# Gate and up of a gated feed-forward block from seven block products per pair of token tiles, with combined weights prepared during attention

## The chip, the cores and the metric

The kernel runs on one core of a Trainium2 chip. The metric is the device time of one launch in microseconds (us); the table below has three runs of it. PE is TensorE, DVE VectorE, ACT ScalarE, POOL GpSimd, SP the engine that issues the DMAs.

## The reference

A transformer layer in float32 on 2048 tokens of width 512: attention with 32 heads of 16 in a sliding window of 256, then a feed-forward part of width 1376 whose gate is a sigmoid.

```
h  = x + attention(layernorm(x), wqkv, wo)
n  = layernorm(h)
h2 = h + (sigmoid(n @ w_gate) * (n @ w_up)) @ w_down
```

## The kernel before

**Tiling.** There are 16 token tiles of 128 (`NT`) and 4 k-tiles of 128 (`KT`). The feed-forward width is cut into columns of 512, 512 and 352 (`CUTS`, L49), called cut 0, 1 and 2 here. To keep float32 accuracy, each operand of the large products is scaled and split into two float16 numbers, hi and lo, and `mm3` (L290 to L293) adds three matmuls for each k-tile: hi·hi, hi·lo and lo·hi. A weight piece is split by `do_split` (L789): ACT writes hi (L796), DVE writes lo (L799).

**Stages.** At first the attention weights are loaded and split (`prep`), x goes into `X`, which stays in SBUF as the residual, and layernorm and the projections of the first tokens run. Attention then goes over 8 blocks of 256 tokens: scores for the row maximum (`do_s`, L593, and the maximum on DVE, L578), scores with keys on partitions (`do_st`, L647 to L658), exponentials on ACT (L623), masks on POOL (L631, L636), the product with the values (`do_pv`, L684), and the output projection, which adds to `X` (`do_wo`, L752). Keys reach their copies through a DRAM buffer (`SK<-mem`). During attention the feed-forward weights are loaded once for their largest entries (`do_amax`), from which the scales of gate, up and down follow (L785).

**Feed-forward.** `do_ln2` (L806) normalizes a token tile, splits it and transposes it by DMA into `x2`, of which eight fit. For a tile and a cut `gu` (L816) makes gate and up, 12 matmuls each, in PSUM rings `s` and `st`; `gated` (L849) takes the sigmoid (L855), multiplies (L859), splits (L246, L253) and transposes by DMA (L871). `do_down` (L874) takes 33 matmuls a tile and adds to the output (L887). Cut 0 of the first four tiles is computed ahead, beside the last attention blocks (`do_early`, L826): its sums are copied to SBUF (L838) and wait there for the sigmoid, since ACT holds the table of the exponential until attention ends (`last exp`).

**Memory.** Buffers of the attention are closed for others: `open_x2` (L905) frees the projection weights for cut 0 of the weights and `x2`; `open_p2` (L916) waits for the last attention products and opens the space for cuts 1 and 2, for down and for what `gated` writes.

**Order.** All engines run fixed instruction streams, written in the order that the class `Planner` (L68) chooses at build time. Each piece of work is a generator that yields its cost on an engine, what it needs and which ring buffers it takes; the planner simulates clocks with these costs and picks, on each engine, what can start earliest, and by a priority among those (`pick`, L151). Priorities are numbers in the table `C` (L55); pieces whose kind is in `alts` may go to more than one engine. All DMAs are issued by SP, in one queue.

## Time and profile before

| what | value |
|---|---|
| three timed runs | 802.03, 800.66, 800.86 us; median 800.86 |
| span of the profiled execution | 800.1 us |
| own time of the profiled execution | given by its span only; the timed runs lie 0.56 to 1.93 us above it |
| granted TensorE clock, mean | 0.996 |
| instructions | 17879 |
| DMA | 87.03 MB, mean 109 GB/s |

The profile is taken in one execution. A matmul's row holds its whole passage through the array, so that rows of matmuls overlap; the pace is read from where consecutive ones start. In a group's row the numbers are total busy us, the mean ns of one, and the idle time of the engine just before, with what ended it.

### The profile page before, as it was taken

The page shows a single profiled execution, that of the slowest core. Times are in us where ns is not written, and L with a number is a line of the kernel's source. Part 1 is how long each engine was busy: PE and PEld are TensorE (multiplying, and loading weights), DVE is VectorE, ACT ScalarE, POOL GpSimd, SP SyncE. Part 2 cuts the span into 40 slices and gives each one's busy share as a digit, 9 for nine tenths or more (in the row PEclk, how much of TensorE's full clock was granted, in tenths as well). Part 3 has the DMA queues.
Part 4 walks back from the last instruction along what each step waited for, and adds up shares of the span by engine and source line. Part 5 has one row for each costly group of instructions (what it writes and reads, how often), then busy time and mean ns, then how long its engine had stood idle before and what let it go on. Part 6 is the DMA issues. An engine that isn't in the chain of part 4 may idle for free.

```text
span 800.1 us, 17879 instructions
## 1 busy us (share of the span) xinstructions
PE 764.1 (95%) x6750; PEld 475.2 (59%) x6750; DVE 486.3 (61%) x1555; ACT 414.3 (52%) x708; POOL 280.1 (35%) x347
## 2 busy tenths in 40 slices
PE   2899999999999999999998999999999999999998
PEld 1567767767777776776665545544444444444443
DVE  5979999988886777766889667732221223222211
ACT  5742878766777777876787765622111111111100
POOL 9730446555455545635478831110000000000000
PEclk9999999999999999999999999999999999999999
DMA  9495565775538534335437466753222232221241
GB/s 326 132 226 171 150 155 130 137 197 127 121 80 123 135 90 102 76 83 117 75 81 136 93 150 172 172 103 63 49 50 50 50 54 49 50 49 39 48 99 40
DMA packets 153927, 87.03 MB, mean 109 GB/s; under 512 B 131120, under 2 KB 133168, under 8 KB 153840
## 3 DMA queue, kind: packets, MB, share of 16 engines
q1 hardware_dynamic: 153840, 85.89, 46.9%
q8 instruction: 53, 0.87, 0.5%
q14 instruction: 34, 0.28, 0.1%
HBM read 31.59 MB, written 10.49 MB: 53 GB/s over the span
## 4 chain that ended last, share of the span: by engine, by line
PE 76%; DVE 10%; issue 4%; DMA 4%; POOL 3%; ACT 2%; SPq 0%; DVEq 0%; POOLq 0%; ACTq 0%
PE mmp L293 27%; PE sp L293 14%; PE stp L293 12%; PE pvp L684 8%; PE sp L593 7%; PE stp L658 2%; PE stp L648 2%; DVE junk L578 2%; DMA SK<-mem 2%; PE stp L647 1%; PE stp L649 1%; DVE sq L514 1%; DMA x<-hl 1%; DVE mq L578 1%; DVE st L423 1%
## 5 line engine op out<-in xcount | busy, mean ns | idle before, releaser
L578 DVE CUSTOM_DVE_ANT_0 junk<-sp,mask 128x320 bf16<-128x320 f32 (+4 forms) x512 | 210.9, 466 | 34.1 <-PE sp L593 32.7
L293 PEld LDWEIGHTS <-x 128*128 128x128 f16 x1152 | 112.0, 98 | 118.3 <-issue 1.8
L623 ACT ACTIVATE pa<-stp,kappa 128x512 f32<-128x512 f32 (+1 forms) x256 | 155.1, 646 | 17.9 <-PE stp L649 15.6
L293 PE MATMUL mmp<-WD,hT 128*128 128x512 f16 (+1 forms) x528 | 130.2, 379 | 0.0
L593 PE MATMUL sp<-SK,SQ 96*128 96x256 f16 (+1 forms) x960 | 122.4, 233 | 6.3 <-DMA SK<-mem 3.0
L293 PE MATMUL mmp<-xT,W 128*128 128x256 f16 x768 | 115.4, 281 | 5.9 <-DVE sq L514 3.9
L593 PEld LDWEIGHTS <-SQ 96*128 96x128 f16 x960 | 78.8, 97 | 28.2 <-issue 11.9
L631 POOL TENSOR_SCALAR_AFFINE_SELECT pa<-pa 128x1024 f32<-128x1024 f32 x56 | 62.0, 1107 | 82.1 <-ACT pa L623 82.1
L623 ACT ACTIVATE pb<-stp,kappa 128x512 f32<-128x512 f32 x128 | 84.2, 685 | 10.5 <-PE stp L658 9.4
L246 ACT ACTIVATE hrow<-e 128x512 f16<-128x512 f32 (+1 forms) x48 | 27.9, 584 | 117.6 <-DVE e L859 116.2
L859 DVE SCALAR_TENSOR_TENSOR e<-stp,e 128x512 f32<-128x512 f32 (+1 forms) x44 | 27.7, 630 | 96.5 <-PE stp L293 96.3
L293 PEld LDWEIGHTS <-hT 128*128 128x128 f16 (+1 forms) x528 | 51.6, 98 | 54.4
L293 PEld LDWEIGHTS <-W 128*128 128x128 f16 x768 | 71.5, 100 | 19.5 <-DVE sq L514 5.2
L430 POOL TENSOR_TENSOR rs<-rs,nhalf 128x1 f32<-128x1 f32 x32 | 19.8, 628 | 155.1 <-DVE rs L427 151.2
L855 ACT ACTIVATE e<-sp,cg 128x512 f32<-128x512 f32 (+1 forms) x44 | 27.9, 634 | 82.9 <-PE sp L293 82.9
L887 DVE SCALAR_TENSOR_TENSOR y<-mmp,cd,X 128x512 f32<-128x512 f32 x16 | 12.0, 751 | 95.5 <-PE mmp L293 95.5
L684 PE MATMUL pvp<-pa,VT 128*17 128x128 f32 (+1 forms) x1408 | 62.5, 307 | 0.0
L648 PE MATMUL stp<-SQ,SK 100*128 100x256 f16 x224 | 59.8, 272 | 0.0
L649 PE MATMUL stp<-SQ,SK 100*128 100x128 f16 x256 | 55.3, 219 | 0.0
L253 POOL TENSOR_TENSOR hl<-xn,hl 128x512 f16<-128x512 f32 x28 | 32.9, 1175 | 55.6 <-ACT hl L246 45.3
L684 PEld LDWEIGHTS pvp<-pa,VT 128*17 128x17 f32 x1408 | 37.7, 97 | 23.4 <-issue 1.8
L647 PE MATMUL stp<-SQ,SK 100*128 100x128 f16 x224 | 49.5, 221 | 2.2 <-ACT pb L623 1.1
(161 smaller groups left out, 1214.2 us busy)
## 6 DMA issues: line engine op xcount, KB each, us to landing
SQ<-sq SPq DMA_DIRECT2D x96, 128.0 KB
SK<-mem SPq DMA_DIRECT2D x16, 384.0 KB
chunk<-in_wd_dram SPq DMA_DIRECT2D x20, 256.0 KB
mem<-sk SPq DMA_DIRECT2D x8, 512.0 KB
chunk<-in_wg_dram SPq DMA_DIRECT2D x16, 256.0 KB
chunk<-in_wu_dram SPq DMA_DIRECT2D x16, 256.0 KB
out_dram<-y SPq DMA_DIRECT2D x16, 256.0 KB
X<-in_x_dram SPq DMA_DIRECT2D x7, 512.0 KB
```

The costliest lines, as they stand in the source:

```text
L246: S.activation(out, x, AF.Copy, scale=scale)
L253: (G if plan.on == POOL_ else V).tensor_tensor(out=out, in0=a, in1=b, op=ALU.subtract)
L293: PE.matmul(ps, a_of(a, k), b_of(b, k), start=(k == 0 and i == 0), stop=(k == n - 1 and i == 2))
L578: V.tensor_tensor_reduce(out=junk[:, c0:], in0=ps[:, c0:], in1=mask[:, c0:], scale=1.0, scalar=-3.0e38, op0=ALU.add, op1=ALU.max, accum_ou ...
L593: PE.matmul(ps[:, col:col + k1 - k0], q, SK[0:96, (2 * a + hf) % 5, 4 * (p % 2) + j, k0:k1], start=True, stop=True)
L623: S.activation(dst, a, AF.Exp, scale=kappa)
L631: G.affine_select(out=f, in_=f, pattern=[[0, 8], [-1, 128]], compare_op=ALU.is_gt, fill=0.0, base=0, channel_multiplier=1)
L647: PE.matmul(a[:, 0:128], ks(k0, g, j), qs(b, g, j, 0, 128), start=True, stop=True)
L648: PE.matmul(a[:, 128:384], ks(k0 + 1, g, j), qs(b, g, j, 0, 256), start=True, stop=True)
L649: PE.matmul(a[:, 384:512], ks(k0 + 3, g, j), qs(b, g, j, 128, 256), start=True, stop=True)
L684: PE.matmul(ps[32 * j:32 * j + 17, u, q0:q1], VT[:, kt % 6, 8 * j + g, :], w[:, j, c:c + q1 - q0], start=first, stop=last, skip_group_chec ...
L855: S.activation(a, g, AF.Sigmoid, scale=cg)
```

## The change

Take two token tiles as the two block rows and the two halves of k as the two block columns of one operand, and on the other side gate and up as block columns over the same halves of k. Gate and up of both tiles are then a 2 x 2 block product, which takes eight block products directly and seven by Strassen's scheme. The change does that for each of 8 pairs of tiles and 3 cuts:

- `do_ln2` handles a pair. Four sums and differences of the normalized tiles are made (DVE or POOL), and the seven left operands are split and transposed in two groups (3 and 4 blocks of 256). Three pairs fit in `X2`, the third only after `open_p2`.
- `do_weights` makes the seven right operands of a cut: differences of gate and up, in powers of two of their scales (`ratio`), on DVE and POOL, and a split of each on ACT and DVE. Cuts 0 and 1 (`AHEAD = 2`) do that during attention; the parts go to DRAM (`WR`) and come back by `do_load` when the space for them opens. Cut 2 is made after `open_p2`.
- `do_pair` runs the seven products, 6 matmuls each. They share three PSUM banks: A takes P1, P6, P7, P4 on top of each other, B takes P5 and P3, C takes P2. Three intermediate values are copied to SBUF (`copied`), three adds join them (`added`); so a product that accumulates waits until the value under it is read. The ring `e` has eight float32 buffers, four a group.
- The rows of `X` of the last eight tiles serve as buffers before their own use: tiles 8 to 11 for the weights, 12 to 15 for x on its way to the first layernorm. x of tiles 4 to 15 is loaded a second time (`load_again`) before the output projection adds to it.
- The order is new: other constants in `C`, other kinds in `alts`, and a list `SHIFT` that moves the priority of each piece by a number of its own.

The core of the diff; the numbers of `C` and all but the first row of `SHIFT` are left out:

```diff
+AHEAD = 2
...
+SHIFT = [
+    -23.88, 385.91, -172.05, -175.74, -69.05, -222.57, -43.03, -68.56, -52.02, -66.89, -89, -90.83, -47.79, -33.13, -87.17, -72.15, -60.27, 9.3, -4.4,
...
         self.count += 1
-        self.submit([prio, self.count, step, piece, next(piece), None])
+        self.submit([prio + shift, self.count, step, piece, next(piece), None, shift])
...
+    RINGS = dict(s=3, st=2, mm=2, pv=1, chunk=3, wl=4, xl=4, ws=8, ln=4, xn=1, hl=1, hlw=2, pp=3, rh=2, rt=2, os=2, whl=1, oT=1, mq=2, mt=2, mem=2,
+                 hl2=1, e=8, hr=3, y=2)
...
+    def load_x(t):
+        late = t >= 4
+        e, *place = yield {DMA_: 0.475}, [("x", t - 1)] if late else [], ["xl"] if late else [], 0.73
+        xs[t] = X[:, NT - 4 + place[0] % 4 if late else t, :], place
+        nc.sync.dma_start(xs[t][0], x[t * P:(t + 1) * P, :])
+        plan.mark(("x", t), e)
+        if not late:
+            plan.mark(("xa", t), e)
+
+    def load_again(t):
+        e, = yield {DMA_: 0.475}, ([("lx", i) for i in range(4, NT)] if t >= NT - 4 else [("parted", c, k) for c in range(AHEAD) for k in range(2)] if t >= NT - 8 else []), [], 1.46
+        nc.sync.dma_start(X[:, t:t + 2, :], x[t * P:(t + 2) * P, :].rearrange("(t p) d -> p t d", p=P))
+        for k in range(t, t + 2):
+            plan.mark(("xa", k), e)
...
+    def do_weights(c, k, prio):
+
+        cols = CUTS[c][1] - CUTS[c][0]
+        ahead = c < AHEAD
+        ring = "wl" if ahead else "ws"
+        x, places, left = [], [], [4]
+        for i, (nm, kk) in enumerate((("g", k), ("u", k), ("g", k + 2), ("u", k + 2))):
+            t, *more = yield {DMA_: 0.5}, [] if i else ["ratio"] if ahead else ["ratio", "p2"], [ring] if ahead else [] if i else [ring] * 4, cols / 700
+            places += more
+            x.append(chunk(wg if nm == "g" else wu, kk, P, c, X[:, NT - 8 + places[i] % 4, :] if ahead else ws[places[i] % 8]))
+            plan.mark(("load", c, k, i), t)
...
+        def part(j, i, scale, needs, last=None):
+            t, *place = yield {ACT_: cols / 1200 + 0.187}, needs, ["chunk"] if ahead else []
+            if ahead:
+                hl = row().bitcast(F16)[:, :2 * cols].rearrange("p (h n) -> p h n", h=2)
+            else:
+                hl = W[c][:, :, j, k, :]
+            S.activation(hl[:, 0, :], x[i], AF.Copy, scale=sc[scale])
+            t, = yield {DVE_: Port(cols / 960 + 0.13)}, [t]
+            V.scalar_tensor_tensor(hl[:, 1, :], x[i], sc[scale], hl[:, 0, :], op0=ALU.mult, op1=ALU.subtract)
...
+            if ahead:
+                t, = yield {DMA_: 0.5}, [t], [], cols / 700
+                if (c, j) not in WR:
+                    WR[c, j] = dram.tile([P, 2, 2, cols], F16, name=f"wr{c}{j}", bufs=1)
+                nc.sync.dma_start(WR[c, j][:, :, k, :], hl)
+                plan.free("chunk", place[0], t)
+                plan.mark(("WR", c, k, j), t)
+
...
+        L = [("load", c, k, i) for i in range(4)]
+        w = lambda j: ("part", c, k, j)
+        for step, piece in enumerate((part(0, 0, "sg", [L[0]]), part(2, 3, "su", [L[3]]), part(1, 2, "sg", [L[2]]),
+                                      less(0, 1, 0, True, "T1", [L[1], w(0)]), less(1, 3, 1, False, "T3", [L[3], ("T1", c, k)]),
+                                      less(3, 3, 0, True, "T2", [("T3", c, k), w(2)]), less(2, 2, 3, False, "T4", [("T2", c, k), w(1)]),
+                                      part(4, 0, "sg", [("T1", c, k), ("T2", c, k)], 0), part(6, 1, "su", [("T3", c, k)], 1),
+                                      part(5, 3, "sg", [("T2", c, k), ("T4", c, k)], 3), part(3, 2, "sg", [("T4", c, k)], 2))):
+            plan.add(prio + 0.02 * step, piece)
...
+    def do_load(c, j):
+        cols = CUTS[c][1] - CUTS[c][0]
+        t, = yield {DMA_: 0.5}, [("WR", c, k, j) for k in range(2)] + ["p2" if c else "x2p"], [], cols / 350
+        nc.sync.dma_start(W[c][:, :, j], WR[c, j])
+        plan.mark(("W", c, j), t)
+
+    ratios = {}
+
+    def do_ratio():
+        t, = yield {DVE_: 0.16}, [("scale", "g"), ("scale", "u")]
+        ratios["r"] = product("ratio", sc["su"], sc["fg"], 2.0 ** -12)
+        plan.mark("ratio", t)
...
+    def do_ln2(p, prio):
+
+        slot = p % 3
+        after = (["p2"] if slot == 2 else []) + ([("x2f", p - 3)] if p > 2 else [])
+        yield {DVE_: 0.0}, ["x2p", ("wo", 2 * p), ("wo", 2 * p + 1)] + after
+        e, (n0, n1), xa = yield from normal(2 * p, [("wo", 2 * p)], "chunk", row, 18, 2)
+        xb = row()
+        plan.mark(("x2n", p, 0), e)
...
+        def combine():
+
+            for i, a, b, op in ((3, 2, 3, ALU.add), (2, 0, 2, ALU.subtract), (0, 3, 0, ALU.subtract), (1, 1, 0, ALU.subtract)):
+                e, = yield alt("less2", POOL_, POOL=0.62, DVE=Port(0.37)), [("x2s", p, 0)]
+                (G if plan.on == POOL_ else V).tensor_tensor(out=A[i], in0=A[a], in1=A[b], op=op)
+            e = yield from both(4, [(xa, 2 * B), (xb, 2 * B)], [e], 1)
...
+    SLOT = ((0, 1), (0, 2), (1, 1), (0, 0), (1, 3), (1, 0), (1, 2))
+    COUNT = 3, 4
+
+    def multiply(ps, p, c, j, first):
+
+        part, at = SLOT[j]
+        n = CUTS[c][1] - CUTS[c][0]
+        for k in range(2):
+            for i, (a, b) in enumerate(((0, 0), (0, 1), (1, 0))):
+                PE.matmul(ps, X2[p % 3][part][:, (a * COUNT[part] + at) * 2 + k, :], W[c][:, b, j, k, :],
+                          start=first and k == 0 and i == 0, stop=k == 1 and i == 2, skip_group_check=not first)
...
+    def do_pair(p, c, prio, early):
+
+        n = CUTS[c][1] - CUTS[c][0]
+        q = ("pair", p, c)
+        bank, value, written = {}, {}, set()
+        rings = dict(A="s", B="s" if early else "st", C="s" if early else "pv")
+        first = [(w, b, g) for w in ("st", "s") for b in (5, 6) for g in range(NG)] if early else ["last exp", "p2"]
+        first += [("hTf", c, 2 * p + i - (6, 4, 4)[c]) for i in range(2) if 2 * p >= (6, 4, 4)[c]]
...
+        F_ = float(2.0 ** -16)
+        evac = {0: [copied("P1", "A", 1.0)], 4: [copied("P5", "B", F_)], 1: [added("g1", "C", "P1", 1.0, ["P2", "copy P1"], True)],
+                5: [copied("P6", "A", F_)], 2: [added("u1", "B", "P6", F_, ["P3", "copy P6"], True)],
+                6: [added("u2", "A", "P5", F_, ["P7", "copy P5"], False)]}
+        waits = {5: "copy P1", 2: "copy P5", 6: "copy P6", 3: "u2"}
+        for i, (j, b) in enumerate(((0, "A"), (4, "B"), (1, "C"), (5, "A"), (2, "B"), (6, "A"), (3, "A"))):
+            needs = ([("W", c, j)] if c < AHEAD else [("part", c, k, j) for k in range(2)]) + [("x2", p, SLOT[j][0])]
+            needs += first if i == 0 else [(waits[j], q)] if j in waits else []
+            fresh = b not in written
+            written.add(b)
+            new = [] if not fresh else [b] if not early else [] if i else ["A", "B", "C"]
+            e, *places = yield {PE_: n / 400 + 0.01}, needs, [rings[x] for x in new] + ["e"] * 4 * (i == 0)
+            if i == 0:
+                for name, at in zip(("P1", "P5", "P6", "P4"), places[-4:]):
+                    value[name] = E8[:, at % 8].bitcast(F32)[:, :n], at
+            for x, place in zip(new, places):
+                t = pvp[0].rearrange("p u q -> p (u q)") if rings[x] == "pv" else psum_tile(rings[x], [P, 512])
+                bank[x] = t[:, :n], place
+            multiply(bank[b][0], p, c, j, fresh)
+            plan.mark((f"P{j + 1}", q), e)
...
```

More of the change, by code (lines that the diff above doesn't have):

```diff
@@ L416, in prep, with normal @@
         plan.mark(("prep", nm), t)
-    def layernorm(t, key, pool, rings, dst, after, more=()):
-        e, n = yield {DVE_: 1.0}, [key], ["ln"]
+    def normal(t, key, ring, tile, shift, n_of=1, ln1=False):
+        e, n = yield {DVE_: 1.0}, key, ["ln"]
+        src = xs[t][0] if ln1 else X[:, t, :]
         st = small.tile([P, 6], F32, name="st6")
-        V.bn_stats(st, X[:, t, :])
+        V.bn_stats(st, src)
         mv = small.tile([P, 2], F32, name="mv")
@@ L759, in tile_block, with chunk @@
     SPANS = CUTS + ((0, D),)
-    def chunk(w, k, r, c):
+    def chunk(w, k, r, c, t=None):
         c0, c1 = SPANS[c]
-        t = chunks.tile([P, 512], F32, name="chunk")
+        t = row() if t is None else t
         nc.sync.dma_start(t[:r, :c1 - c0], w[k * P:k * P + r, c0:c1])
@@ L785, in do_amax, with halves @@
             V.tensor_reduce(out=mx, in_=am[nm], axis=AX.X, op=ALU.max)
-            t = yield from scale(nm, mx, t)
+            t = yield from scale(nm, mx, t, 13 if nm == "d" else 12)
             plan.mark(("scale", nm), t)
-    def do_split(nm, n):
-        w, k, r, c = pieces[nm][n]
-        cols = SPANS[c][1] - SPANS[c][0]
-        t, place = yield {DMA_: 0.5}, [("scale", nm), "p2" if c else "x2p"], ["chunk"], cols / 700
+    def halves(hi, lo, x, w, cols, needs):
+        t, = yield {ACT_: cols / 1200 + 0.187}, needs
+        S.activation(hi, x, AF.Copy, scale=w)
+        t, = yield {DVE_: Port(cols / 960 + 0.13)}, [t]
+        V.scalar_tensor_tensor(lo, x, w, hi, op0=ALU.mult, op1=ALU.subtract)
+        return t
@@ L793, in do_split @@
+    def do_split(n):
+        w, k, r, c = pieces["d"][n]
+        t, place = yield {DMA_: 0.5}, [("scale", "d"), "p2"] + [("parted", c, k) for c in range(AHEAD, 3) for k in range(2)], ["chunk"], D / 700
         x = chunk(w, k, r, c)
-        hi, lo = (W[nm, c][:r, h, k, :] for h in range(2))
-        t, = yield {ACT_: cols / 1200 + 0.187}, [t]
-        S.activation(hi, x, AF.Copy, scale=sc["s" + nm][:r])
-        t, = yield {DVE_: Port(cols / 960 + 0.13)}, [t]
+        hi, lo = (W["d"][:r, h, k, :] for h in range(2))
+        t = yield from halves(hi, lo, x, sc["sd"][:r], D, [t])
@@ L851, in gated @@
+    def gated(t, c, g, eg, u, eu, ps=None):
         n = CUTS[c][1] - CUTS[c][0]
         m = PADDED[c]
-        e, ne = yield {ACT_: n / 1200 + 0.145}, [eg, "last exp", "p2"], ["e"]
-        a = p2.tile([P, 512], F32, name="e", bufs=RINGS["e"])[:, :n]
-        S.activation(a, g, AF.Sigmoid, scale=cg)
-        if ng is not None:
-            plan.free("s", ng, e)
-        e, = yield {DVE_: n / 960 + 0.069}, [e, eu]
-        V.scalar_tensor_tensor(a, u, float(2.0 ** -18), a, op0=ALU.mult, op1=ALU.mult)
@@ L860, in gated @@
-        if nu is not None:
-            plan.free("st", nu, e)
-        e, nh = yield alt("hhi", ACT_, ACT=n / 1200 + 0.093, DVE=Port(n / 1920 + 0.069)), [e], [f"h{c}"]
-        h = hrow[c][nh % len(hrow[c])]
+        e, = yield {ACT_: n / 1200 + 0.145}, [eg, "last exp", "p2"]
+        a = g[0]
+        S.activation(a, ps[0] if ps else a, AF.Sigmoid, scale=cg)
+        if ps:
+            plan.free("s", ps[1], e)
+        e, = yield alt("gate", DVE_, DVE=Port(n / 960 + 0.069), POOL=n * 0.0021 + 0.08), [e, eu]
@@ L890, in do_down @@
         nc.sync.dma_start(out[t * P:(t + 1) * P, :], y)
-    work = kappa = x2p = p2 = cg = cd = None
-    hrow = {}
+    work = kappa = cg = cd = hl2 = ws = hr = hTs = None
     def open_work():
@@ L910, in open_x2 @@
         qkv.close()
-        x2p = ctx.enter_context(tc.tile_pool(name="x2p", bufs=2, side="left", reuse_waits="tile"))
-        for nm in "gu":
-            W[nm, 0] = x2p.tile([P, 2, KT, CUTS[0][1]], F16, name="W0" + nm, bufs=1)
+        pool = ctx.enter_context(tc.tile_pool(name="x2p", bufs=1, side="left", reuse_waits="tile"))
+        weights(pool, 0)
+        hl2 = pool.tile([P, 8 * B], F16, name="hl2")
+        for i in range(2):
+            x2_slot(pool, i)
         plan.mark("x2p", e)
@@ L925, in open_p2 @@
[L925 to L932 removed]
+        pool = ctx.enter_context(tc.tile_pool(name="p2", bufs=1, side="right", reuse_waits="tile"))
```

264 lines of the change are left out of this document (161 added, 103 removed), and 27 rows, old and new, of the table SHIFT.

## The prediction

> **What bounds the kernel now.** I read the page first: the header, the busy line and the line on the chain that ended last.
>
> ```profile
> span 800.1 us, 17879 instructions
> ...
> PE 764.1 (95%) x6750; PEld 475.2 (59%) x6750; DVE 486.3 (61%) x1555; ACT 414.3 (52%) x708; POOL 280.1 (35%) x347
> ...
> PE 76%; DVE 10%; issue 4%; DMA 4%; POOL 3%; ACT 2%; SPq 0%; DVEq 0%; POOLq 0%; ACTq 0%
> ```
>
> TensorE is busy for 95% of the span and carries 76% of the chain. These are averages over unlike stages, so the view by windows came second. Its columns are busy us and instruction counts of PE, weight loads, DVE, ACT, POOL, then granted clock, DMA share and GB/s.
>
> ```profile
> 0.00:80.00 80.00, 57.79 (x437) 42.45 (x438) 65.79 (x219) 42.06 (x77) 42.44 (x53) 0.98 0.71 214
> 80.00:160.00 80.00, 77.71 (x966) 59.03 (x964) 79.10 (x323) 62.90 (x120) 41.22 (x56) 1.00 0.60 143
> 160.00:240.00 80.00, 77.33 (x974) 58.41 (x972) 68.80 (x258) 56.55 (x95) 41.32 (x52) 0.98 0.57 131
> 240.00:320.00 80.00, 79.56 (x1040) 59.16 (x1038) 59.41 (x232) 59.58 (x99) 42.35 (x53) 1.00 0.56 112
> 320.00:400.00 80.00, 79.59 (x994) 58.32 (x991) 58.80 (x227) 62.06 (x103) 42.23 (x53) 1.00 0.43 88
> 400.00:480.00 80.00, 75.67 (x770) 43.10 (x769) 62.62 (x154) 60.48 (x101) 56.82 (x67) 1.00 0.55 115
> 480.00:520.00 40.00, 40.00 (x217) 21.04 (x215) 28.64 (x49) 25.02 (x43) 5.44 (x5) 1.00 0.71 173
> 520.00:768.00 248.00, 248.00 (x1240) 120.99 (x1239) 59.04 (x94) 45.16 (x74) 8.25 (x9) 1.00 0.28 55
> 768.00:800.00 32.00, 28.40 (x132) 12.67 (x130) 4.05 (x6) 0.50 (x1) 0.00 (x0) 1.00 0.26 69
> ```
>
> The reader is to see three stages. Up to 80 us the kernel starts up, and PE idles 22.2 us. From 80 to 480 it does attention: PE idles 2.29, 2.67, 0.44, 0.41 and 4.33 us in the five windows, 10.1 in all, while DVE is nearly as full as PE at first (79.10 of 80) and has 74% from 240 to 400. From 480 on gate, up and down follow, and PE has no idle time until the last 3.6 us; DVE works 24% and ACT 18% of 520:768.
>
> A busy PE need not be PE at its pace, so the third view was the chain in order of time: three pieces from the last stage.
>
> ```profile
> 508.93 2.59 PE stp L293 x12
> 511.52 1.79 PE sp L293 x12
> 767.90 28.52 PE mmp L293 x132
> ```
>
> Twelve matmuls of 512 columns take 2.59 us, 0.216 each; twelve of 352 take 1.79, 0.149 each; the 132 at the end hold 0.216 without a break. They follow each other at the rate of their columns, so what leaves PE in this stage leaves the span, as long as nothing else becomes late.
>
> **The change part by part.**
>
> *Matmuls removed.* Both halves of the work are counted by these groups (384 matmuls for gate and up of each cut, 192 each):
>
> ```profile
> L293 PE MATMUL sp<-W1g,x 128*128 128x512 f16 x192 | 44.7, 379 | 0.9 <-DVE W1g L799 0.9
> L293 PE MATMUL sp<-W2g,x 128*128 128x352 f16 x192 | 37.9, 312 | 0.0
> ```
>
> Two tiles and one cut need 48 matmuls now. After, seven products of two k-tiles and three hi/lo terms need 42. There are 8 pairs and 3 cuts: 144 matmuls go, 96 of 512 columns (20.7 us) and 48 of 352 (7.2): **-27.9 us**, an eighth of 223. Each matmul keeps its own weight load, so no new load appears.
>
> *More evacuation.* Now a group has sigmoid, multiply, hi and lo for each tile; after come three copies out of PSUM and three adds for each pair and cut. The nearest rows:
>
> ```profile
> L855 ACT ACTIVATE e<-sp,cg 128x512 f32<-128x512 f32 x28 | 19.1, 683 | 33.5 <-PE sp L293 33.5
> L859 DVE SCALAR_TENSOR_TENSOR e<-stp,e 128x512 f32<-128x512 f32 x28 | 19.3, 691 | 87.8 <-PE stp L293 87.8
> L859 DVE SCALAR_TENSOR_TENSOR e<-stp,e 128x352 f32<-128x352 f32 x16 | 8.4, 524 | 8.7 <-PE stp L293 8.5
> ```
>
> A pair adds 12 x 0.69 + 6 x 0.52 = 11.4 us to DVE and ACT. It takes 42.1 us of PE now (96 x 0.216 + 48 x 0.149 + 66 for down x 0.216) and 38.6 after. DVE's 24% are 10 us a pair; with all of the new work 21.5 of 38.6. Hidden by PE, in bulk. In order it isn't free: bank A takes P1, P6, P7, P4, and P7 waits for the copy of P6, P4 for the add that reads P7. The planner can put pieces of down there, 14.3 us a pair, 4.7 a group. I take **+1** for what is left, bounds 0 and the second rival.
>
> *Weights made early.* The cuts 0 and 1 are now split into 28 parts (7 products, 2 k, 2 cuts), each one ACT and one DVE instruction, after eight differences with a ratio on DVE and eight plain ones on POOL. Gate of cut 0 was split between 424.6 and 443.1 us, of cut 1 between 472.8 and 483.6; now all of it needs the scale of up, so lies behind 168 us by this trace.
>
> ```profile
> L785 DVE TENSOR_REDUCE mxw<-amu x1: 170/170/170, 167.9 to 167.9; 128x1 f32<-128x16 f32 x1
> ...
> L799 DVE SCALAR_TENSOR_TENSOR W0g<-chunk,sg,W0g x4: 739/934/1652, 424.6 to 443.1; 128x512 f16<-128x512 f32 x4
> L799 DVE SCALAR_TENSOR_TENSOR W1g<-chunk,sg,W1g x4: 739/740/746, 472.8 to 483.6; 128x512 f16<-128x512 f32 x4
> ...
> L799 DVE SCALAR_TENSOR_TENSOR W0g<-chunk,sg,W0g 128x512 f16<-128x512 f32 x4 | 4.3, 1065 | 0.0
> L799 DVE SCALAR_TENSOR_TENSOR W0u<-chunk,su,W0u 128x512 f16<-128x512 f32 x4 | 4.0, 1009 | 0.5 <-ACT W0u L796 0.5
> L799 DVE SCALAR_TENSOR_TENSOR W1g<-chunk,sg,W1g 128x512 f16<-128x512 f32 x4 | 3.0, 742 | 0.0
> L796 ACT ACTIVATE W0g<-chunk,sg 128x512 f16<-128x512 f32 x4 | 2.9, 716 | 0.0
> L253 POOL TENSOR_TENSOR hl<-xn,hl 128x512 f16<-128x512 f32 x28 | 32.9, 1175 | 55.6 <-ACT hl L246 45.3
> ```
>
> DVE in attention gets 28 x 0.742 + 8 x 0.69 - 8.3 (cut 0, gone) = 18 us at the price of the quiet rows, 28 x 1.065 + 8 x 1.065 - 8.3 = 30 at that of W0g; I take 24. The same instruction takes 742 ns where POOL works 5.44 of 40 us, and 1065 in a window where it works 56.82 of 80. The Trainium skill, page "SBUF — State Buffer", section "Who interferes with whom", says that a VectorE instruction with two inputs in SBUF and a GpSimd instruction that reads SBUF exclude each other; by that rule the eight POOL differences are paid on DVE too, as an estimate up to 8 x 1.175 = 9.4 us, which would make the first rival below 807 at its full price in place of 798. The two rows agree with the rule, without telling which POOL instruction held which.
>
> From 160 to 400 DVE works 68.80 + 59.41 + 58.80 = 187.0 of 240 us; with 24 it has 211, 88%. The window that has 86% now is 160:240, with 2.67 us of idle PE in 80; at that rate 240 us idle 8.0, against 2.67 + 0.44 + 0.41 = 3.5 now: **+4.5**. Bounds 0 (the spare 53 us take it all) and +24 (PE waits for each of them). ACT gets 20 x 0.716 = 14.3 us in 178.2 of 240; that fits.
>
> *Through DRAM.* 28 stores and 14 loads back move 7.3 MB each way, and reloading x for 12 tiles adds 3.1: 17.7 MB. The start moves 214 GB/s at a share of 0.71, which is 301 GB/s of full engines, so they cost 59 us of all sixteen; 160:400 has 0.52 of 240, 125 us. 184 of 240 still fits. But SP's one queue carries them too, ahead of key loads like this, which PE waited for:
>
> ```profile
> 264.86 4.85 DMA SK<-mem
> ```
>
> A 256 KB transfer ahead of one costs 0.87 us at 301 GB/s. None to eight such meetings: **+1**, bounds 0 and 7.
>
> *Around the last attention block.* Cut 1 comes back from DRAM in place of 8 splits; cut 2 has 14 parts of 352 columns in place of 8; down's 11 are unchanged. A new wait: the eight float buffers are all taken by the two early pairs, so the next group stands behind their gating, which needs the last exponential, the table load of sigmoid and a sigmoid, multiply, hi and lo.
>
> ```profile
> L855 ACT ACT_TABLE_LOAD x1 | 1.3, 1283 | 0.0
> L246 ACT ACTIVATE hrow<-e 128x512 f16<-128x512 f32 x32 | 20.0, 628 | 69.6 <-DVE e L859 68.2 <-DMA hT<-hrow 1.4
> L253 DVE TENSOR_TENSOR hrow<-e,hrow 128x512 f16<-128x512 f32 x32 | 22.7, 710 | 15.6 <-ACT hrow L246 15.5
> ```
>
> 1.28 + 0.68 + 0.69 + 0.63 + 0.71 = 4.0, and 2.7 more for the second tile: 6.7 us, covered if the second early pair (42 x 0.216 = 9.1 us) runs then. Against that stand 4.33 us of idle in 400:480 that may go. **+1**, bounds -4.3 and +6.7. Queued behind the waiting gates on ACT and DVE is only the next evacuation.
>
> *New order.* Each piece gets a shift of its own. PE's idle time up to 480 is 32 us, most of it at the start, where weights and x must land and be split whatever the order. **-2**, bounds -8 and +5, since no row prices an order. At the end nothing changes: down's last matmuls still run alone.
>
> Sum: 800.1 - 27.9 + 1 + 4.5 + 1 + 1 - 2 = 777.7 of span. The runs before have a median of 800.86, 0.76 above the span: **778.5 us**.
>
> **The rivals.** *One: attention gives most of it back.* If PE waits for all of DVE's 24 us instead of 4.5, the time is 798.0; half way, 788. For it: DVE is on the chain with 10%, and is full from 80 to 160. Against: in 240:400 its share is 74%, and scores have three PSUM buffers before PE feels it.
>
> *Two: slower, since P4 waits.* From P7's last matmul to P4's first:
>
> ```profile
> 572.96 2.75 PE L293 MATMUL sp<-W0g,x 128*128 128x512 f16 x12
> 575.81 0.69 ACT L855 ACTIVATE e<-sp,cg 128x512 f32<-128x512 f32 x1 [1.53 <-PE sp L293]
> 428.56 1.26 ACT L623 ACTIVATE pb<-stp,kappa 128x512 f32<-128x512 f32 x2
> 429.87 0.22 PE L647 MATMUL stp<-SQ,SK 100*128 100x128 f16 x1 [0.20 <-ACT pb L623]
> ```
>
> The twelve end 0.16 us after their 2.59; the reader starts 0.10 later; the add takes 0.69; and PE resumes 0.05 after its releaser (428.56 + 1.26 to 429.87). That is 1.00 us, 0.83 for 352 columns. Uncovered in all 24 groups: 16 x 1.00 + 8 x 0.83 = 22.6. With one DVE instruction ahead of the add (0.69 or 0.52) it is 16 x 1.69 + 8 x 1.35 = 37.8, and the time 778.5 - 1 + 37.8 = 815.3. It decides from (800.86 - 777.5) / 24 = 0.97 us a group. Against: 4.7 us of down a group to put there.
>
> PE's gaps and its clock stand side by side in these windows:
>
> ```profile
> 20.00:40.00 20.00, 16.45 (x100) 11.43 (x99) 18.75 (x39) 15.30 (x28) 14.15 (x14) 0.91 0.43 132
> 420.00:440.00 20.00, 17.70 (x210) 10.09 (x209) 18.97 (x40) 15.37 (x28) 16.96 (x21) 1.00 0.75 136
> ```
>
> 3.55 us of idle came with a clock of 0.91, 2.30 with 1.00. The Trainium skill, page "TensorE: Matmul & The Clock Gate", section "A second HAM failure mode: psum-queue depth-cycling", tells of a kernel whose cycling through PSUM banks left PE small gaps and made its clock fall again and again, which speaks against this change. The 420:440 row doesn't bear that out for gaps of this size; the rival keeps its chance for the waits alone.
>
> *Three: the new order takes out the start's idle as well*, or attention absorbs all and the transition's gaps close: below 765 (778.5 - 4.5 - 5.3 - 2 - 3 = 763.7). Against: 160:240 shows that a fuller DVE does leave PE gaps.
>
> That the change doesn't do what it says I leave out: the loops fix 42 for 48.
>
> **How the numbers follow.** Forecast 0.80, rival one 0.11, two 0.05, three 0.04. The low end takes the free ends of attention (-4.5), DMA (-1), waits (-1) and transition (-5.3), and -2 of the order's: 765. The high end takes 17 of attention's 19.5 further us: 796. Within 0.2% (1.6 us, about what can be told from no change here) lies the full price of rival one in part: 0.03. Faster 0.92, slower 0.05.
>
> **What would show it.** Matmul instructions 6606 instead of 6750. In the last stage PE without idle time and a pair in 38.6 us: step one right. PE waiting for a DVE add or a copy there, over 0.97 us a group: rival two. DVE above 85% between 160 and 400 with PE idle 6 to 10 us: the price of early weights right; with 20 or more: rival one. The prediction is wrong if attention ends over 15 us later than now, if the last stage is PE-idle, or if the first 80 us shrink by more than 5.

## The result, and the profile after

The changed kernel has a median of 787.85 us (787.53 to 787.97, 4 runs), the kernel before 801.44 on the same chip (800.66 to 802.24, 4 runs): a ratio of 0.9837, 95% interval 0.9814 to 0.9861. That is 13.6 us less, where the prediction had 22.4 less. Its profiled run has a span of 786.1 us, 14.0 less than before. Header, busy line and chain of the changed kernel:

```profile
span 786.1 us, 17989 instructions
...
PE 743.5 (95%) x6606; PEld 460.9 (59%) x6606; DVE 557.9 (71%) x1682; ACT 460.7 (59%) x801; POOL 320.6 (41%) x390
...
PE 64%; DVE 12%; issue 8%; ACT 7%; DMA 5%; POOL 3%; DVEq 0%; POOLq 0%; ACTq 0%; SPq 0%
```

The 144 matmuls are gone as foretold (6750 to 6606). They were worth 27.9 us, but PE's busy time fell by only 764.1 - 743.5 = 20.6, and its idle time rose from 800.1 - 764.1 = 36.0 to 42.6. So 7.3 us came back as matmuls that are busy without being at their pace, and 6.6 as idle time: 27.9 - 7.3 - 6.6 = 14.0. PE's share of the chain fell from 76% to 64%. The windows say where (columns as in the prediction):

```profile
0.00:80.00 80.00, 59.74 (x455) 43.02 (x456) 62.22 (x225) 42.92 (x77) 41.98 (x52) 0.98 0.71 222
80.00:160.00 80.00, 75.87 (x925) 56.42 (x924) 75.97 (x312) 60.13 (x115) 39.01 (x54) 0.98 0.52 116
160.00:240.00 80.00, 78.86 (x1022) 59.97 (x1023) 69.78 (x260) 60.27 (x99) 38.63 (x51) 1.00 0.66 150
240.00:320.00 80.00, 77.83 (x959) 57.62 (x949) 74.88 (x253) 64.34 (x108) 43.75 (x52) 1.00 0.91 208
320.00:400.00 80.00, 78.22 (x1004) 55.76 (x1003) 71.96 (x244) 66.53 (x112) 43.56 (x53) 1.00 0.79 199
400.00:480.00 80.00, 74.57 (x783) 43.41 (x781) 54.25 (x143) 56.45 (x93) 53.95 (x65) 1.00 0.54 110
480.00:520.00 40.00, 37.18 (x177) 17.71 (x178) 35.46 (x59) 24.76 (x46) 16.08 (x17) 0.96 0.96 201
520.00:768.00 248.00, 246.85 (x1235) 120.69 (x1234) 111.12 (x190) 85.26 (x157) 43.58 (x49) 1.00 0.38 75
```

From 520 on PE idles 1.15 us in 248. From 160 to 400 it idles 1.14 + 2.17 + 1.78 = 5.1 (before 3.5). The stretch that was full before, 480:520, now has 2.82 us idle, 177 matmuls where there were 217, and a clock of 0.96.

Because busy time hides slow matmuls, I also priced every matmul by its columns: 0.215 us for 512 in float16, the rest in proportion; float32 at half that pace, and the four matmuls of P.V (the product with the values, `do_pv`) that run side by side as one, since such fours of 256 columns start 0.216 us apart. What a stretch takes beyond that is lost. The table is worked out from the matmul rows of each trace; its columns add up to the span. Two experiments, described below, stand beside it: 21 of 24 is the kernel before with an eighth of its products left out, short supply is the changed kernel with little work to make weights.

| us | before | after | 21 of 24 | after, again | short supply |
|---|---|---|---|---|---|
| matmuls by their columns | 724.9 | 697.2 | 697.2 | 697.2 | 697.2 |
| lost up to the first P.V product | 34.4 | 31.9 | 31.9 | 32.6 | 32.3 |
| lost from there to 160 us | 8.6 | 13.3 | 8.8 | 13.5 | 13.8 |
| lost from 160 to 250 | 8.7 | 7.9 | 8.5 | 9.2 | 8.9 |
| lost from 250 to 400 | 8.6 | 13.0 | 9.2 | 13.2 | 8.9 |
| lost from 400 to the last P.V product | 8.2 | 7.0 | 9.2 | 7.7 | 6.6 |
| lost in the next 100 us | 1.7 | 10.8 | 3.6 | 9.4 | 4.8 |
| lost in the rest | 5.0 | 5.0 | 4.9 | 5.0 | 5.1 |
| span | 800.1 | 786.1 | 773.3 | 787.8 | 777.6 |

Of the 27.7 us of matmuls, attention (the four rows between the first and the last P.V product) lost 7.1 more than before and the 100 us behind it 9.1 more; the start lost 2.5 less. Attention's loss stands in two places: 4.4 us from 250 to 400, where the weights of cuts 0 and 1 are made (the lo parts, L889, run from 254.0 to 393.9 us), and 4.7 before 160 us, where none is made yet; its other two rows lost 2.0 less. The chain of the changed kernel behind attention, in order of time:

```profile
471.88 1.28 ACT L1067
473.17 1.33 ACT SQ L1067 x2
...
476.32 0.93 DVE hr L288 x2
...
479.16 1.74 DVE W L889 x2
...
492.57 0.97 POOL chunk L980
493.61 0.90 POOL chunk L980
...
496.40 0.93 POOL WD L288
497.36 1.44 DVE WD L908
498.80 0.50 DVE W L889
499.30 0.66 DVE X L813
499.96 0.51 DVE W L889
500.47 0.61 DVE SQ L1021
501.12 2.72 PE sp L998 x6
```

Until 501 the work that ends last isn't PE's. Read backwards: a product waits for an add (L1021) that DVE reaches only after two lo parts of cut 2 (L889) and an update of x (L813); these stand behind a difference (L908), which waits for one on POOL (L288), and that one is queued behind the combinations of the next pair's x (L980). At its start the chain runs through the gating of the early pairs: the table load and sigmoids on ACT (L1067) and the lo parts of the gated values on DVE (L288). In the chain of before, 508.93 and 511.52, PE carried it. What PE itself waited for between 400 and 560 us (engine, line, releaser, us in total, times, longest):

```profile
PE stp L998 <- DMA W<-wr: 2.6, 1, 2.6
PE sp L998 <- DVE SQ L1021: 2.1, 1, 2.1
PE pvp L998 <- DMA W<-wr: 1.4, 1, 1.4
PE stp L998 <- ACT SQ L281: 1.2, 1, 1.2
```

Two products wait for weights that come back from DRAM, one for the add, one for a copy out of PSUM: 7.3 us in four waits with three kinds of releaser.

### The profile page after: what moved, and what is told of

The parts are those of the page before. It is cut to its first block, busy times and chain, and to the rows that moved or that the text cites. A ratio compares the mean times of both kernels' runs of the same rounds, so it can differ in the third digit from the quotient of the medians.

```text
span 786.1 us, 17989 instructions
## 1 busy us (share of the span) xinstructions
PE 743.5 (95%) x6606; PEld 460.9 (59%) x6606; DVE 557.9 (71%) x1682; ACT 460.7 (59%) x801; POOL 320.6 (41%) x390
## 4 chain that ended last, share of the span: by engine, by line
PE 64%; DVE 12%; issue 8%; ACT 7%; DMA 5%; POOL 3%; DVEq 0%; POOLq 0%; ACTq 0%; SPq 0%
PE mmp L328 24%; PE sp L998 13%; PE pvp L745 7%; PE sp L654 6%; PE stp L998 5%; DVE junk L639 3%; PE pvp L998 2%; PE stp L719 2%; PE stp L709 2%; DMA oT<-whl 2%; DMA x<-hl 2%; PE stp L708 1%; ACT pa L684 1%; DVE mq L639 1%; PE stp L710 1%
## 5 line engine op out<-in xcount | busy, mean ns | idle before, releaser
L639 DVE CUSTOM_DVE_ANT_0 junk<-sp,mask 128x320 bf16<-128x320 f32 (+4 forms) x512 | 207.4, 464 | 13.7 <-PE sp L654 13.3
L998 PEld LDWEIGHTS <-x 128*128 128x128 f16 x1008 | 98.2, 98 | 105.1 <-issue 5.4
L998 PE MATMUL sp<-W,x 128*128 128x512 f16 (+1 forms) x612 | 133.2, 361 | 2.1 <-DVE SQ L1021 2.1
L654 PE MATMUL sp<-SK,SQ 96*128 96x256 f16 (+2 forms) x960 | 127.2, 232 | 5.8 <-DVE mq L639 2.7
L328 PE MATMUL mmp<-xT,W 128*128 128x256 f16 x768 | 111.6, 277 | 5.6 <-DVE W L454 2.2
L654 PEld LDWEIGHTS <-SQ 96*128 96x128 f16 x960 | 80.9, 97 | 34.8 <-issue 16.1
L684 ACT ACTIVATE pb<-stp,kappa 128x512 f32<-128x512 f32 x128 | 83.0, 685 | 13.5 <-PE stp L719 12.2
L281 ACT ACTIVATE SQ<-sp 128x512 f32<-128x512 f32 (+1 forms) x45 | 24.4, 544 | 80.1 <-PE sp L998 79.7
L998 PE MATMUL stp<-W,x 128*128 128x512 f16 (+1 forms) x264 | 57.4, 355 | 3.8 <-DMA W<-wr 2.6
L709 PE MATMUL stp<-SQ,SK 100*128 100x256 f16 x224 | 59.2, 271 | 0.0
L1099 DVE SCALAR_TENSOR_TENSOR RH<-mmp,cd,X 128x512 f32<-128x512 f32 x16 | 11.9, 750 | 60.1 <-PE mmp L328 60.1
L328 PE MATMUL mmp<-WO,oT 128*128 128x512 f16 x192 | 49.9, 381 | 0.9 <-DMA oT<-whl 0.8
L328 PE MATMUL mmp<-W,xT 128*128 128x512 f16 x192 | 48.9, 378 | 0.2 <-DVE sk L575 0.2
L719 PE MATMUL stp<-SQ,SK 100*128 100x256 f16 x256 | 46.8, 274 | 1.4 <-ACT pa L684 0.8
```

The source lines that it names most:

```text
L281: S.activation(out, x, AF.Copy, scale=scale)
L328: PE.matmul(ps, a_of(a, k), b_of(b, k), start=(k == 0 and i == 0), stop=(k == n - 1 and i == 2))
L639: V.tensor_tensor_reduce(out=junk[:, c0:], in0=ps[:, c0:], in1=mask[:, c0:], scale=1.0, scalar=-3.0e38, op0=ALU.add, op1=ALU.max, accum_ou ...
L654: PE.matmul(ps[:, col:col + k1 - k0], q, SK[0:96, (2 * a + hf) % 5, 4 * (p % 2) + j, k0:k1], start=True, stop=True)
L684: S.activation(dst, a, AF.Exp, scale=kappa)
L709: PE.matmul(a[:, 128:384], ks(k0 + 1, g, j), qs(b, g, j, 0, 256), start=True, stop=True)
```

## The experiments

The first theory: the product stage runs at PE's pace, so the matmuls removed are worth their columns, and the missing 9 us come from supplying the weights, partly in attention, partly right behind it. Rivals: evacuation in bank A, the DRAM traffic, or the order itself.

**An eighth product put back.** P4 is run twice, which gives 48 matmuls a group with all else as in the changed kernel; P4 then counts double in the output.

```
-        for k in range(2):
+        for k in (0, 0, 1, 1) if j == 3 else (0, 1):
```

> The changed kernel with each group's last product run twice (twelve matmuls in place of six, the sums are then not the reference's): PE gets its 144 matmuls back, 27.9 us, everything else and every order stays. Theory (the product stages are bound by PE, the added copies and adds are hidden): 25 to 28 us over the changed kernel, 813 to 816, a little less than 27.9 only if some fall into PE's gaps around the last attention block. Rival (PE waits for copies and adds inside a group, so that the saved matmuls were partly replaced by waits): additional work on PE hides such waits, 10 to 18 us over it.

814.51 us (812.67 to 816.85), ratio 1.0168 [1.0134, 1.0202]. Against the changed kernel's 0.9837 that is 0.0331 of 801, 26.5 us, for 27.7 by columns. Its last stage shows what PE does there:

```profile
520.00:768.00 248.00, 248.00 (x1242) 121.27 (x1241) 104.46 (x184) 82.19 (x151) 42.35 (x50) 1.00 0.35 73
```

PE is full: an added product is paid nearly in full. Whether a removed one is earned in full, the next run asks from the other side. With eight products the change would be 13.5 us slower than before; that is the price of all the rest.

**The kernel before with 21 of 24.** The last k-tile of up is left out in the kernel before, so its output lacks that part; the matmul count is that of the changed kernel.

```
-            mm3(ps, ..., k, KT)
+            if nm == "g" or k < KT - 1:
+                mm3(ps, ..., k, KT if nm == "g" else KT - 1)
```

> The kernel before, leaving out the three matmuls of the last k-tile of up in each tile and cut (so up is short of a quarter of its sum): 144 matmuls or 27.9 us less on PE, and nothing of the rest of the change. Theory: 27 to 28 us faster than before, about 773.5; the difference to the changed kernel, about 14 us, is then the price of all the rest of the change. Rival (without these matmuls the stage runs into another bound, whatever the change does): 15 to 22 us faster.

774.89 us (773.65 to 776.67), ratio 0.9674 [0.9638, 0.971], 26.1 us less than before.

```profile
PE 735.2 (95%) x6606; PEld 459.4 (59%) x6606; DVE 483.3 (63%) x1555; ACT 413.8 (54%) x708; POOL 280.5 (36%) x347
```

With the same 6606 matmuls PE is busy 735.2 us here and 743.5 in the changed kernel, and idle 38.1 and 42.6: 8.3 + 4.5 = 12.8 us. From both sides the matmuls are worth 26 to 27 us and the rest costs 13.

**The add in bank A twice.** The add u2 that frees bank A for P4 is issued two times (up counts P7 double): 16 x 0.69 + 8 x 0.52 = 15.2 us more DVE.

```
-                V.scalar_tensor_tensor(y, bank[which][0], factor, y, op0=ALU.mult, op1=ALU.add)
+                for _ in range(2 if name == "u2" else 1):
+                    V.scalar_tensor_tensor(y, bank[which][0], factor, y, op0=ALU.mult, op1=ALU.add)
```

> The changed kernel with the add between the seventh product and the fourth issued twice in each of the 24 groups (the value is then wrong), 0.69 us more (0.53 in cut 2) on the way from P7 to P4, 15.3 us in all; orders unchanged. Theory (pieces of down or of another group stand there): 0 to 3 us slower, all of it in the groups around the last attention block. Rival (P4 waits exposed): 12 to 16 us slower.

794.17 us (792.67 to 798.96), ratio 0.9926 [0.9901, 0.995]: about 7 us over the changed kernel, between the two expectations. The waits of PE:

```profile
PE sp L998 <- DVE SQ L1022: 5.2, 10, 2.9
```

Ten stops in place of one, 3.1 us more. Eight of the ten stand in the product stage, 1.7 us in all. So the cover has an end. For the other 4 us I have no cause: attention's last product ends at 475.2 us here and at 469.0 in the changed kernel, though few of these adds stand before it, and two traces of the changed kernel alone differ by 3 us in this (below).

**Cut 1's reload first.** Cut 1's seven loads from DRAM get a priority ahead of all else; cut 0's keep theirs.

```
-                plan.add(C["ld"] + 7 * c + i, do_load(c, j))
+                plan.add(C["ld"] + 7 * c + i - 5000 * c, do_load(c, j))
```

> The changed kernel with the loads that bring cut 1's weights back from DRAM put ahead of the raw loads of cut 2 in SP's queue (a priority alone; the order up to there is the same). In the changed kernel's trace PE waits 2.63 and 1.36 us for them at 475 and 479 us. Theory (these waits are part of the price around the last attention block): 2 to 4 us faster, 784 to 786. Rival (PE would there wait for cut 2's weights or a full VectorE instead, so the time only moves): within 1 us of the changed kernel.

802.61 us (799.86 to 804.25), ratio 1.0009 [0.999, 1.0028]: 14 us slower than the changed kernel, and no expectation allowed for that. SP's queue, a wait on PE's timeline and a window:

```profile
470.74 4.87 SPq L926 DMA_DIRECT2D W<-wr  x7
```

```profile
498.56 4.13 PE L328 MATMUL mmp<-WO,oT 128*128 128x512 f16 x12 [4.54 <-DMA oT<-whl]
```

```profile
480.00:500.00 20.00, 12.51 (x52) 4.99 (x51) 18.97 (x28) 9.03 (x18) 12.76 (x13) 0.95 0.94 220
```

Seven loads in a row hold SP's queue for 4.87 us; in the changed kernel raw loads and transposes stand between them. The last three transposes of attention's output (oT) that SP issues by 496 us start at 467.98, 482.20 and 495.47, against 466.54, 477.25 and 489.33 in the changed kernel, and PE waits 4.54 us for the third. It works 12.51 of 20 us there. A second wait, of a kind that the changed kernel doesn't have behind 560 us, stands in the product stage, for a copy by ACT:

```profile
598.83 1.05 PE L998 MATMUL sp<-W,x 128*128 128x352 f16 x6 [3.73 <-ACT SQ L281]
```

These two are 8.3 of the 14 us; the rest isn't traced to a cause. Being early with one input makes another late.

**One supply at a time.** Each of the next four takes work or bytes away, so the weights that the products read are incomplete; the instructions of PE stay. *Short early split*: for the cuts 0 and 1 the lo parts and the differences treat 64 columns instead of 512.

```
+            m = 64 if ahead else cols
-            V.scalar_tensor_tensor(hl[:, 1, :], x[i], sc[scale], hl[:, 0, :], op0=ALU.mult, op1=ALU.subtract)
+            V.scalar_tensor_tensor(hl[:, 1, :m], x[i][:, :m], sc[scale], hl[:, 0, :m], op0=ALU.mult, op1=ALU.subtract)
```

> The changed kernel with the VectorE and GpSimd work of the early weights cut short: lo parts and differences of cuts 0 and 1 are computed for 64 columns in place of 512, and hi is stored in lo's place (the product is then not the reference's). ACT's work, all DMAs and all orders stay. It takes some 17 to 25 us from VectorE between 160 and 400 us. Theory (the prediction's term of 4.5 us is VectorE's early work): 3 to 6 us faster than the changed kernel, 782 to 785, with the last attention product that much earlier than 469 us. Rival (attention doesn't feel it; its gaps come from transfers or the order): within 1.5 us.

786.53 us (783.79 to 788.44), ratio 0.9829 [0.9797, 0.9862].

*Small DRAM traffic*: only the hi half is stored and half of that loaded; the products read this quarter in place of all four.

```
-                nc.sync.dma_start(WR[c, j][:, :, k, :], hl)
+                nc.sync.dma_start(WR[c, j][:, 0:1, k, :], hl[:, 0:1])
...
-        nc.sync.dma_start(W[c][:, :, j], WR[c, j])
+        nc.sync.dma_start(W[c][:, 0:1, j, 0:1], WR[c, j][:, 0:1, 0:1])
```

> The changed kernel with less traffic through DRAM for cuts 0 and 1: of each part only hi is stored, and only hi of one k-tile is loaded back and used for all (the product is then not the reference's): 3.7 MB in place of 7.3 out, 1.8 in place of 7.3 back. Work of the engines and all orders stay. Theory (1 us in attention, and the waits of 4 us for cut 1's weights): 2 to 6 us faster than the changed kernel. Rival (the bytes are the main price of attention as well): 8 us faster or more; or, if bytes cost nothing, within 1.5 us.

786.6 us (786.41 to 787.28), ratio 0.9834 [0.981, 0.9858].

*Short cut 2*: the first of these edits with `not ahead`, so for cut 2 alone, whose hi half the products read twice.

> The changed kernel with the lo parts and the differences of cut 2 computed for 64 columns in place of 352, hi used in lo's place (not the reference's product): some 6 to 10 us less on VectorE and 3 on GpSimd between 477 and 507 us, where VectorE is busy for 18.83 of 20. Theory after the run with the reload put first (a full VectorE is one part of the price behind the last attention block): 2 to 5 us faster than the changed kernel. Rival (supply of bytes alone limits that stretch): within 1.5 us.

789.8 us (788.39 to 790.09), ratio 0.9874 [0.9845, 0.9903].

*Small reload*: only a quarter of cut 1 comes back, and the products read that; cut 0 is as it was.

```
-        nc.sync.dma_start(W[c][:, :, j], WR[c, j])
+        nc.sync.dma_start(W[c][:, :, j] if c == 0 else W[c][:, 0:1, j, 0:1], WR[c, j] if c == 0 else WR[c, j][:, 0:1, 0:1])
```

> The changed kernel with only a quarter of cut 1's weights loaded back from DRAM (hi of one k-tile, used for all; not the reference's product): 0.9 in place of 3.7 MB between 469 and 492 us, orders unchanged. Theory (that stretch, whose transfers take 1.10 of what sixteen engines have, is short of bytes): 3 to 6 us faster than the changed kernel. Rival (it is short of VectorE instead): within 1.5 us.

788.88 us (787.82 to 790.47), ratio 0.9863 [0.9836, 0.989].

None of the four differs from the changed kernel (0.9837 [0.9814, 0.9861]) by more than the intervals. The waits of PE from 400 to 560 say why, for short cut 2 and for the small reload:

```profile
PE stp L1001 <- DMA W<-wr: 2.5, 1, 2.5
PE mmp L328 <- DMA oT<-whl: 2.2, 3, 1.5
PE pvp L1001 <- DMA W<-wr: 1.3, 1, 1.3
```

```profile
PE sp L998 <- DVE SQ L1021: 2.7, 1, 2.7
PE stp L998 <- ACT SQ L281: 2.4, 2, 1.5
PE sp L998 <- ACT SQ L281: 1.7, 1, 1.7
```

Without DVE's work for cut 2 the 2.1 us for the add are nearly gone, and 2.2 for a transpose stand there beside the weights. Without the bytes of cut 1 the 4.0 for weights are gone, and the waits for the add and for ACT's copies have grown from 3.3 to 6.8. So it looks as if the inputs of this stretch arrive within 2 to 3 us of each other, and PE waits for whichever is last.

In attention two of the four do show, though, where the early weights are made. From 250 to 400, priced as in the table, the short early split lost 10.8 us and the small DRAM traffic 10.1. Six traces in which the early weights are those of the changed kernel (its own two, the reload put first, short cut 2, the small reload and the next experiment) lost 12.3 to 13.5. Each edit thus takes 2 to 3 us away there; in the time of the whole kernel that is within the intervals.

**No wait in bank A.** Outside the early groups the copy of P6 and the add of u2 read bank C, which no later product of the group writes, so P7 and P4 follow at once. Those two then take P2 in place of P6 and P7.

```
-            copy(value[name][0], bank[which][0], factor)
+            copy(value[name][0], bank["C" if name == "P6" and not early else which][0], factor)
...
-                V.scalar_tensor_tensor(y, bank[which][0], factor, y, op0=ALU.mult, op1=ALU.add)
+                V.scalar_tensor_tensor(y, bank["C" if name == "u2" and not early else which][0], factor, y, op0=ALU.mult, op1=ALU.add)
```

> The changed kernel with the copy of P6 and the add behind P7 reading bank C in place of bank A, except in the two early groups (the values are then not the reference's): same instructions, sizes and orders, but P7 no longer waits for that copy, nor P4 for that add. Theory (right behind the last attention block no piece of down is there to stand between, so these handovers are exposed, about a microsecond a group in some six to nine groups): 3 to 7 us faster than the changed kernel, with PE's idle time from 469 to 531 us falling from 9.4 to about 4. Rival (PE's gaps there come from late operands, not from the group's own chain): within 1.5 us.

788.17 us (786.47 to 791.98), ratio 0.9858 [0.9823, 0.9893]: nothing gained. PE's idle time from 469 to 531 us is 6.5 us here and 6.7 in the changed kernel (not 9.4, as the expectations have it). The waits for the add and the copy that stood there are gone, but those for a transpose have grown from 0.8 to 3.5:

```profile
PE mmp L328 <- DMA oT<-whl: 3.5, 3, 2.3
```

So the evacuation in bank A alone doesn't hold this stretch. That it costs nothing there isn't shown, since another late input took its place.

**The changed kernel again, and all supply short at once.** The second has the short lo parts and differences in all three cuts and the small DRAM traffic together; both ran on one chip.

> The changed kernel once more, on the chip of the other three, so that they are compared with it and not with another chip's: 0.981 to 0.986 of the time before, and the same idle times of PE by stage as in its first profile within 2 us.

> The changed kernel with all of the cheap-supply edits at once: lo parts and differences of the seven operands for 64 columns in all three cuts, half the bytes stored and a quarter loaded back, hi used for lo (not the reference's product); orders and ACT's work stay. Theory (the supply of weights is only the smaller part of the price): 3 to 6 us faster than the changed kernel, about 3 of it before the last attention product, and at least 5 us of the 9.4 us idle behind it still there. Rival (the single edits moved little since one late operand took the place of the other; all at once they free the stretch): 8 us faster or more, with idle time behind the last attention product below 3 us.

The changed kernel: 787.7 us (786.03 to 789.49), ratio 0.9846 [0.9822, 0.987]. All short: 779.07 us (777.57 to 779.3), ratio 0.9734 [0.9714, 0.9753], 8.6 us less. One window of the first, then of the second:

```profile
480.00:520.00 40.00, 35.28 (x175) 17.01 (x176) 36.95 (x62) 25.67 (x50) 16.22 (x17) 1.00 1.00 215
```

```profile
480.00:520.00 40.00, 40.00 (x209) 20.32 (x208) 33.27 (x62) 27.96 (x52) 11.22 (x14) 1.00 0.87 174
```

From 480 to 520 PE is full again. From 469 to 531 it idles 1.7 us, for 7.0 in the first. So both parts of the rival came: over 8 us, and idle time there below 3. The chain of the second in that stretch is PE's, where the changed kernel's was DVE's and POOL's:

```profile
477.41 1.46 PE sp L998 x6
478.87 2.59 PE mmp L328 x12
481.46 1.30 PE sp L998 x6
```

By the table, the 100 us behind attention lost 4.6 us less, and 250 to 400 lost 4.3 less, which is nearly what it had lost more than before. The windows of that stretch, before, changed and with short supply, show it in PE's idle time (0.85, 3.60, 0.80):

```profile
250.00:400.00 150.00, 149.15 (x1896) 109.85 (x1894) 112.08 (x434) 113.34 (x187) 80.20 (x101) 1.00 0.49 98
```

```profile
250.00:400.00 150.00, 146.40 (x1830) 105.39 (x1828) 137.11 (x454) 122.86 (x206) 80.99 (x97) 1.00 0.87 207
```

```profile
250.00:400.00 150.00, 149.20 (x1871) 108.45 (x1870) 124.35 (x473) 127.40 (x212) 73.31 (x100) 1.00 0.74 175
```

So the supply does hold the time, but as several limits side by side: taken away singly they gave 1 us or nothing, taken away together 8.6. Against 21 of 24 (0.9674) 0.006 of 801, some 5 us, are left. By the table they stand before 160 us (13.8 for 8.8), ahead of the gating, of the adds and of the x for pairs. What costs them there (the order, the x that is loaded twice, other rings) no run tells.

**No shifts.** The list of shifts is emptied, so that the order follows the plain priorities.

> The changed kernel with all of the per-piece shifts of priority at zero, the constants of the order as changed: what the order alone is worth. Theory (an order decides about PE's idle time, not about its work, and the constants go with the shifts): 10 to 40 us slower than the changed kernel, all of it idle PE. Rival (the order is worth 2 us, as the prediction put it): 1 to 4 us slower.

892.37 us (890.54 to 898.35), ratio 1.1179 [1.1133, 1.1224]: some 105 us over the changed kernel, far beyond both expectations. A wait of PE and two windows:

```profile
PE mmp L299 <- DMA oT<-whl: 24.5, 3, 22.3
```

```profile
418.00:441.80 23.80, 23.24 (x137) 15.63 (x137) 22.54 (x98) 11.32 (x18) 5.82 (x8) 0.50 0.36 69
441.80:469.00 27.20, 24.41 (x291) 16.49 (x288) 20.42 (x76) 18.50 (x32) 17.28 (x23) 1.00 0.82 220
```

One wait of 22.3 us for a transpose (until 588 us), attention ending at 553.0 us, and a granted clock of 0.50 for 23.8 us in which PE counts as busy for 23.24, with 137 matmuls; the next 27.2 us have 291 at 1.00. Of the 102.7 us that the span is longer than the changed kernel's, 54.7 are idle PE and 48.0 are matmuls that are busy without being at their pace, so "all of it idle PE" was wrong as well. The plain priorities alone are no order for this kernel. This doesn't tell what the new list is worth against the old one: the two kernels have different pieces, and the old list can't be laid over the new ones.

## Why the prediction was partly right

*Matmuls removed (-27.9).* Right. Added back they cost 26.5, taken from the kernel before they give 26.1, and the product stage runs at PE's pace.

*More evacuation (+1, bounds 0 and rival two).* Right in the product stage. From 520 to 768 PE idles 1.15 us with DVE at 111.12 and ACT at 85.26 of 248, and the rest behind those 100 us lost 5.0 us before and after. Right behind attention it isn't shown to be free: PE waits there for an add (2.1 us) and a copy (1.2), and without these waits a transpose took their place. Rival two's mechanism exists but not its size: of 24 doubled adds ten reached PE, for 5.2 us.

*Weights made early (+4.5) and through DRAM (+1).* Right in size where the weights are made: 250 to 400 lost 4.4 us more, 5.5 were forecast, and with the supply short 4.3 of them are gone. That all of attention lost 7.1, not far from 5.5 either, is a coincidence: 4.7 of it stand before 160 us, ahead of the first early weight, where the prediction had no term. Its way to the price was only half right: it read the price as idle time and named 6 to 10 us of it in 160:400 as the sign; the idle time there is 5.1 for 3.5 before, a rise of 1.6, and the larger part of the loss is busy time that isn't at pace. DVE worked 69.78 + 74.88 + 71.96 = 216.6 of 240, 90%, for 88% foretold. What was added, by the groups between 168 and 470 us:

```profile
L889 DVE SCALAR_TENSOR_TENSOR chunk<-X,sg,chunk 128x512 f16<-128x512 f32 x20 | 16.1, 815 | 4.9 <-ACT chunk L887 4.9
L908 DVE SCALAR_TENSOR_TENSOR X<-X,ratio 128x512 f32<-128x512 f32 x8 | 7.2, 902 | 1.4 <-POOL X L288 1.4
L889 DVE SCALAR_TENSOR_TENSOR chunk<-X,su,chunk 128x512 f16<-128x512 f32 x8 | 6.0, 746 | 0.0
```

16.1 + 7.2 + 6.0 - 8.3 = 21.0 us where I took 24 from 18 to 30. The means of one form differ, 815 and 746, as they did before. (The row of 742 ns in the prediction stands at 472.8 to 483.6 us, so only in part in the window named beside it.) Of the 28 lo parts in these two groups, 17 ran while POOL did nothing and took 736 to 752 ns; of the 11 that ran beside a POOL instruction, nine took 737 to 769 and two 1143 and 1754. The Trainium skill, page "SBUF — State Buffer", section "Who interferes with whom", says that a VectorE instruction with two inputs in SBUF contends with a GpSimd instruction that reads SBUF. The trace agrees in that only instructions beside POOL are long, and it shows that most beside POOL are not. The DMA share of 240:320 rose to 0.91, where 184 of 240 (0.77) was foretold for the mean; the mean is (0.66 + 0.91 + 0.79) / 3 = 0.79. How the 4.4 us divide between VectorE's work and the traffic stays open: either edit alone takes 2 to 3 us away there, both together all of it.

*Around the last attention block (+1, bounds -4.3 and +6.7).* Here the prediction failed: the stretch lost 9.1 us more, beyond the bound; 6.9 of that is idle PE. The step priced one new wait, the gating of the early pairs (4.0 to 6.7 us), and thought the second early pair would cover it, and it thought the 4.33 us of idle in 400:480 might go. They rose to 5.43. PE's waits there don't name the gating but weights from DRAM (4.0), an add (2.1) and a copy (1.2); the chain does run through the gating before it comes to the lo parts of cut 2, and no run took it away. The step did list the causes, the reload in place of splits and 14 parts of cut 2 for 8, and put no price on them. But DVE had 28.64 of 40 us in 480:520 before and has 35.46 now, and the adds stand in DVE's queue behind lo parts. No piece of down covers a late input there (its first matmul stands at 527.76; before at 518.83, where little was late). DVE's spare time in that window is what I should have asked for. All supply short took 4.6 us of it away (9.4 to 4.8), so this cause is shown for about half; the rest, with the gating, the x of the next pairs on POOL and the order among the candidates, stays open.

*New order (-2, bounds -8 and +5).* The start lost 2.5 us less; but the kernel before with 21 of 24 also loses 31.9 there, so this can't be put down to the new order. From the first P.V product to 160 us 4.7 us more are lost, in all traces of the changed kernel and its variants with the same shifts (13.1 to 13.9 for 8.6), and in 80:160 PE idles 4.13 us for 2.29. Whether that is the order or the x that passes through other buffers, no run tells. A gain from the order isn't seen.

The sum: -2.5 + 7.1 + 9.1 - 27.7 = -14.0 of span, against -22.4. Rival one's place was partly right, for attention did give back, but 7.1 us and not 24; that the time is the 788 which the prediction gives for half of rival one is a coincidence, since the larger part was lost behind attention. Rival three's did not come: no stretch but the start closed its gaps.

On the clock, three windows of 3.4 us of the changed kernel:

```profile
473.80:477.20 3.40, 1.45 (x7) 0.48 (x5) 2.88 (x5) 3.40 (x8) 0.00 (x0) 1.00 0.93 302
...
497.70:501.10 3.40, 1.31 (x7) 0.49 (x5) 3.40 (x6) 1.35 (x4) 1.92 (x2) 1.00 0.63 121
501.10:504.50 3.40, 3.38 (x9) 1.14 (x9) 1.87 (x2) 2.72 (x7) 2.27 (x2) 0.50 0.01 2
```

The 0.96 of the window 480:520 is an average: the clock was 0.50 for 3.4 us and 1.00 else. These 3.4 us begin where the wait of 2.1 us for the add ends. At half the pace they cost 1.7 us, as an estimate, which agrees with the second trace of the changed kernel: there the clock stays at 1.00, and the matmuls behind attention that are busy without being at their pace take 1.3 us, for 3.0 in the first. So a late input can cost more than its wait. But idle time alone doesn't decide it: 473.80:477.20 has 1.95 us of it, for 2.09 in 497.70:501.10, and is followed by a clock of 1.00. The product stage that cycles through banks has 1.00 from 520 to 768, so the new use of banks, gone through 24 times, takes no toll on the clock there.

## What to carry to other kernels

Price a saving from both sides: put the removed work back into the new kernel, and take as much out of the old. Here that gave 26 to 27 us and left 13 to look for. Then cut the loss by time before you compare it with a forecast: a total that agrees can stand elsewhere. Where two stages meet, ask of each engine and queue how full that very stretch is before you price a new piece there at nothing. If an edit that removes one wait gains nothing, look at which wait has taken its place before calling that cost free, and remove all of them together once.
